# Attention output with V as the TensorE weights on four 128x32 column tiles, denominators in a second pass, and the projections of the same stages on column tiles

## The chip, the cores and the metric

The kernel runs on one core of one Trainium2 chip. The metric is the device time of one execution in microseconds (us). Three executions of the kernel before took 690.76, 691.12 and 691.33 us; their median is 691.12 us.

## What is computed

The reference is one transformer block in bfloat16 on 2048 tokens of width 1024: layernorm, attention with a sliding window, a residual, a second layernorm, a feed-forward layer with silu, and a residual. The attention has 32 heads of 32 channels, and each query sees itself and the 255 tokens before it.

```
qkv = layernorm(x) @ wqkv            # 1024 -> 3 * 1024
scores = q @ k.T * 32 ** -0.5        # per head
mask = (i - j >= 0) & (i - j < 256)  # i query, j key
p = softmax(where(mask, scores, -1e9))
h = x + (p @ v) @ wo
out = h + silu(layernorm(h) @ w1) @ w2   # w1: 1024 x 3584
```

## The kernel before

Tokens are handled in four blocks of 512 (b = 0 to 3). Heads are handled in groups of four (g = 0 to 7), because four heads of 32 channels fill the 128 partitions. After the projections of block 0 the kernel runs four **streamed stages** and then the feed-forward layer. In streamed stage b (0 to 3) the attention of block b is computed in small pieces between the matmuls of a dense projection: q, k and v of block b + 1 in stages 0 to 2, and the output projection `wo` of blocks 0 to 2 in stage 3. A stage has 24 dense groups of 8 matmuls, 128x128 weights by 512 columns (`v_group` L235, `qk_group` L244, `wo_group` L266; matmuls at L240, L250, L271), so 192 dense steps. Each dense group accumulates in one of two PSUM banks, `acc0` and `acc1`, and ends in one VectorE (DVE) instruction that empties the bank (L242, L252, L273).

The order of all engines is written out by hand (a manual schedule): each engine executes its instructions in the order in which the program emits them. Ahead of each dense step `Stream.between` (L434) is called. When a burst is due it first emits one waiting attention piece, then the burst of score matmuls, and then the dense step. Stage 0 has 16 bursts, so one comes every 12 dense steps; the stages after it have 20, five for each two head groups (one `scores_c` and four `scores_xy`), so one comes every 9.6 dense steps.

Score matmuls (L303, L329, L355) have the keys as weights, on tiles of 32 rows by 64 or 128 columns, and leave scores with keys on partitions and queries along the free dimension. ScalarE (ACT) takes exp of them into SBUF rings (L315, L316, L337, L363 to L365): `xy_ring` with two slots for each parity of the head group, and `c_ring` with three slots. GpSimd (POOL) then zeroes the triangles outside the window (`select`, L371 and L373).

The **attention output** of a head group (`attn_out`, L377; matmul at L383) has the probabilities as weights, 128x128, and V as the moving operand with 33 columns: 32 channels and a column of ones, so that column 33 of the result is the softmax denominator. Each group takes 48 such matmuls (16 outputs by three key tiles; 36 in block 0). The results for two heads lie in one PSUM bank (`o_ps`), with queries on partitions. `attn_norm` (L392) divides: a reciprocal of the 128x8 denominators (L394) and a multiplication of 128x256 (L395) into `obuf`. Then `attn_transpose` (L401) sends `obuf` through a DMA transpose on the SyncE (SP) queue to `qT`, where channels are on partitions, as `wo` needs them. There are two `o_ps` banks, one for each pair of heads.

In the last stage the pieces that remain are emitted between the first groups of the feed-forward layer. Layernorms are also emitted step by step between dense groups: that of block 2 in stage 0, that of block 3 in stage 1, none in stage 2, and the second layernorm of block 0 in stage 3.

Of the kernel before, what the change touches and what calls it, by code (L numbers as in the profile page):

```python
# [8 lines left out]
BF16 = mybir.dt.bfloat16  # L9
F32 = mybir.dt.float32  # L10
# [16 lines left out]
CHUNKS = [  # L27
    [(-2, "X", 0), (-1, "C", 0), (0, "X", 1)],
    [(-1, "Y", 0), (0, "X", 2), (1, "Y", 1)],
    [(0, "X", 3), (1, "Y", 2), (2, "X", 4)],  # L30
    [(1, "Y", 3), (2, "C", 1), (3, "Y", 4)],
]


CHUNKS_0 = [
    [(0, "X", 0)],
    [(0, "X", 1), (1, "Y", 0)],
    [(0, "X", 2), (1, "Y", 1), (2, "X", 3)],
    [(1, "Y", 2), (2, "C", 1), (3, "Y", 3)],
]  # L40
SPLIT = [(0, 8), (8, 16), (16, 21), (21, 27), (27, 32)]
# [3 lines left out]
def kernel(  # L45
# [23 lines left out]
    VW = DH + 1  # L69
# [15 lines left out]
    r_a = big.tile([P, 49664], BF16, name="r_a")  # L85
    r_e = big.tile([P, 13312], BF16, name="r_e")
    r_n = big.tile([P, 1536], BF16, name="r_n")
# [4 lines left out]
    o_ps = [ps.tile([P, 8, 64], F32, name=f"o_ps{i}") for i in range(2)]  # L92
# [24 lines left out]
    v = view(r_a, 32768, S // P, H, VW)  # L117
# [6 lines left out]
    obuf = [view(r_n, 512 * i, 4, P) for i in range(3)]  # L124
# [36 lines left out]
    nc.gpsimd.memset(v[:, :, :, DH:VW], 1.0)  # L161
# [4 lines left out]
    def busy(n):  # L166
        nc.tensor.matmul(o_ps[0][:].rearrange("p (a c) b -> p a (c b)", c=2)[:, 0:n], lhsT=warm, rhs=wide[:, 0:n], start=True, stop=True)  # L167
# [67 lines left out]
    def v_group(b, j, c, copy, between=None):  # L235
        acc = next_acc()
        for kt in range(KT):
            if between:
                between(kt)
            nc.tensor.matmul(acc, lhsT=lnT_b[b % 2][:, kt, j * P:(j + 1) * P], rhs=wv[:, kt, c * 512:(c + 1) * 512],  # L240
                             start=(kt == 0), stop=(kt == KT - 1))
        copy(out=v[:, b * 4 + j, c * 16:(c + 1) * 16, 0:DH], in_=acc.rearrange("p (h d) -> p h d", d=DH))  # L242

    def qk_group(b, which, g, copy, between=None):  # L244
        acc = next_acc()
        col0 = which * D + g * P
        for kt in range(KT):
            if between:
                between(kt)
            nc.tensor.matmul(acc, lhsT=wqk[:, kt, col0:col0 + P], rhs=lnT_b[b % 2][:, kt, :],  # L250
                             start=(kt == 0), stop=(kt == KT - 1))
        copy(out=(qT, kT)[which][b][:, g, :], in_=acc)  # L252
# [13 lines left out]
    def wo_group(b, j, c, between=None):  # L266
        acc = next_acc()
        for g in range(G):
            if between:
                between(g)  # L270
            nc.tensor.matmul(acc, lhsT=qT[b][:, g, j * P:(j + 1) * P], rhs=wo[:, g, c * 512:(c + 1) * 512],  # L271
                             start=(g == 0), stop=(g == G - 1))
        nc.vector.tensor_tensor(out=t_out[j % 2][:, c * 512:(c + 1) * 512], in0=acc,  # L273
                                in1=r_in[(b * 4 + j) % 6][:, c * 512:(c + 1) * 512], op=ALU.add)
        if c == 1:
            late.append(lambda: nc.sync.dma_start(out=h_dram[(b * 4 + j) * P:(b * 4 + j + 1) * P, :], in_=t_out[j % 2]))


    def chunk_of(i, bank, piece, pair, hh):
        if bank == "C":  # L280
            return c_ring[:, (i + 1) % 3, pair * 2 + hh, piece * P:(piece + 1) * P]
        if i < G:
            c0 = hh * 512 + piece * P
        else:
            c0 = 1024 + hh * P if piece == 2 else hh * 512 + (piece - piece // 3) * P
        return xy_ring[(i % 2 * 2 + "XY".index(bank)) * 2 + pair][:, c0:c0 + P]

    def scores_xy(b, g, odd):
# [20 lines left out]
        for pair in range(2):  # L309
            e = xy_ring[((b * G + g) % 2 * 2 + odd) * 2 + pair]  # L310
            tri = e[:, 0:1024].rearrange("p (h c q) -> p h c q", h=2, q=256)
            bank = sc[pair]
            both = bank[:, :, 0:192]
            both = bass.AP(tensor=both.tensor, offset=both.offset, ap=[*both.ap[:2], [320, 2], both.ap[2]])
            nc.scalar.activation(out=tri[:, :, :, 64:256], in_=both, func=ACT.Exp, scale=scale)  # L315
            nc.scalar.activation(out=e[:, 1024:1280].rearrange("p (h q) -> p h q", q=P), in_=bank[:, :, 192:320], func=ACT.Exp, scale=scale)  # L316
            four = e[:, 0:1024].rearrange("p (c q) -> p c q", q=256)
            select(four[:, :, 0:P], four[:, :, 64:64 + P], False)
            select(four[:, :, P:2 * P], four[:, :, P:2 * P], True)

# [19 lines left out]
    def scores_0(g, odd):  # L340
# [20 lines left out]
        for pair in range(2):  # L361
# [7 lines left out]
            select(e[:, :, 384:512], e[:, :, 384:512], True)  # L369

# [6 lines left out]
    def attn_out(b, g, first, last):  # L377
        i = b * G + g
        for n in range(first, last):
            pair, qt, hh = n // 8, n // 2 % 4, n % 2  # L380
            chunks = (CHUNKS if b else CHUNKS_0)[qt]
            for m, (kt, bank, piece) in enumerate(chunks):
                nc.tensor.matmul(  # L383
                    o_ps[pair][:, qt * 2 + hh, 0:VW],
                    lhsT=chunk_of(i, bank, piece, pair, hh),
                    rhs=v[:, b * 4 + kt, g * 4 + pair * 2 + hh, :],
                    start=(m == 0), stop=(m == len(chunks) - 1),
                )
            if n % 8 == 7:
                attn_norm(i, pair)  # L390

    def attn_norm(i, pair):  # L392
        recip = small.tile([P, 8, 1], F32, name="recip", tag="recip")
        nc.vector.reciprocal(out=recip[:], in_=o_ps[pair][:, :, DH:VW])  # L394
        nc.vector.tensor_tensor(  # L395
            out=obuf[i % 3][:, :, pair * 64:(pair + 1) * 64].rearrange("p t (h d) -> p t h d", d=DH),
            in0=o_ps[pair][:, :, 0:DH].rearrange("p (t h) d -> p t h d", h=2),
            in1=recip[:].rearrange("p (t h) o -> p t h o", h=2).to_broadcast([P, 4, 2, DH]), op=ALU.mult,
        )

    def attn_transpose(b, g):  # L401
        i = b * G + g
        nc.sync.dma_start_transpose(out=qT[b][:, g, :].rearrange("p (t q) -> p t q", q=P),
                                    in_=obuf[i % 3].rearrange("p t d -> p (t d)"))

    def attn_piece(b, g, first, last):

        for k in range(2):
            a, z = max(first - 16 * k, 0), min(last - 16 * k, 16)
            if a < z:  # L410
                attn_out(b, g + k, a, z)
                if z == 16:
                    late.append(lambda k=k: attn_transpose(b, g + k))

    class Stream:
# [3 lines left out]
        def __init__(self, b):  # L419
# [4 lines left out]
            for g in range(0, G, 2):  # L424
                if b:
                    self.bursts += [lambda g=g: scores_c(b, g)]
                    self.bursts += [lambda g=g, k=k, o=o: scores_xy(b, g + k, o) for k in range(2) for o in range(2)]
                    self.pieces += [lambda g=g, s=s: attn_piece(b, g, *s) for s in SPLIT]
                else:
                    self.bursts += [lambda g=g, k=k, o=o: scores_0(g + k, o) for k in range(2) for o in range(2)]  # L430
                    self.pieces += [lambda g=g, k=k: attn_piece(b, g, k, k + 8) for k in range(0, 32, 8)]
            self.n = len(self.bursts)

        def between(self, kt):  # L434
# [8 lines left out]
            self.seen += 1  # L443

# [37 lines left out]
    acc_banks += [o[:].rearrange("p a b -> p (a b)") for o in o_ps]  # L482
# [47 lines left out]
    for j in range(2):  # L530
        nc.scalar.activation(out=v[:, j, 16:32, 0:DH], in_=pair[j].rearrange("p (h d) -> p h d", d=DH), func=ACT.Identity, scale=rs[:, j:j + 1])
# [60 lines left out]
    dense = [lambda j=j, c=c: v_group(1, j, c, dve, stream.between) for j in range(4) for c in range(2)]  # L592
    dense += [lambda w=w, g=g: qk_group(1, w, g, dve, stream.between) for g in range(G) for w in range(2)]
# [10 lines left out]
    for b in range(2, NB):  # L604
        stream = Stream(b - 1)
        dense = [lambda j=j, c=c: v_group(b, j, c, dve, stream.between) for j in range(4) for c in range(2)]
        dense += [lambda w=w, g=g: qk_group(b, w, g, dve, stream.between) for g in range(G) for w in range(2)]
# [31 lines left out]
    for n in range(24):  # L639
# [3 lines left out]
        wo_group(*dense[n], stream.between)  # L643
# [5 lines left out]
        if n == 17:  # L649
            nc.sync.dma_start(out=w2[0], in_=w2_v[:, 0:4, :])  # L650
# [3 lines left out]
    pending += coming  # L654
# [27 lines left out]
    load_w2(5)  # L682
    for b in range(NB):
        extra = []
        if b == 0:
            extra = [(f, 1) for f in pending]
            pending = []
        for ft in range(FT):
            acc = h1_group(b, ft)
            run_late()  # L690
            if extra:
                extra.pop(0)[0]()
# [3 lines left out]
            silu(b, acc, ft)  # L696
            if b == 0 and 7 <= ft < 15:
# [61 lines left out]
```

## Time and profile before

| what | value |
|---|---|
| median of 3 runs (lowest to highest) | 691.12 us (690.76 to 691.33) |
| span of the profiled execution, first to last instruction | 688.9 us |
| PE (matmul) busy | 685.2 us, 6011 matmuls |
| DVE busy | 291.2 us |
| ACT busy | 244.2 us |
| POOL busy | 160.8 us |
| attention output matmuls, L383 | 1440 |
| score selects on POOL, L373 | 288, 157.8 us |
| attention transposes through DMA | 32, 2.3 us from issue to landing |

The profile is of one execution. Its own time is its span; the time that a run reports is measured around it, and the median of the runs is 2.2 us above this span. Busy time of PE counts an instruction from its start to its modelled end, and matmuls overlap, so a busy PE can still lose time between the starts of two matmuls. PEld stands for the loads of weights, which run beside matmuls.

### The profile page before, as it was taken

The page shows a single profiled execution, that of the slowest core. Times are in us where ns is not written, and L with a number is a line of the kernel's source. Part 1 is how long each engine was busy: PE and PEld are TensorE (multiplying, and loading weights), DVE is VectorE, ACT ScalarE, POOL GpSimd, SP SyncE. Part 2 cuts the span into 40 slices and gives each one's busy share as a digit, 9 for nine tenths or more (in the row PEclk, how much of TensorE's full clock was granted, in tenths as well). Part 3 has the DMA queues.
Part 4 walks back from the last instruction along what each step waited for, and adds up shares of the span by engine and source line. Part 5 has one row for each costly group of instructions (what it writes and reads, how often), then busy time and mean ns, then how long its engine had stood idle before and what let it go on. Part 6 is the DMA issues. An engine that isn't in the chain of part 4 may idle for free.

```text
span 688.9 us, 14243 instructions
## 1 busy us (share of the span) xinstructions
PE 685.2 (99%) x6011; PEld 342.3 (50%) x6011; DVE 291.2 (42%) x613; ACT 244.2 (35%) x464; POOL 160.8 (23%) x295
## 2 busy tenths in 40 slices
PE   9999999999999999999999999999999999999998
PEld 4445555555555555544444444444444444444445
DVE  5267647744444449444316133342233251333111
ACT  7326666666667666421300033300133100233000
POOL 1006666566666656400000000000000000000000
PEclk9999999999999999999999999999999999999999
DMA  7832231126241889871023310022300123100110
GB/s 259 275 64 69 40 85 57 25 63 186 71 131 21 257 252 272 199 267 40 23 88 112 84 39 0 1 91 70 85 0 1 21 96 90 39 1 1 30 39 24
DMA packets 78641, 61.48 MB, mean 89 GB/s; under 512 B 52465, under 2 KB 62705, under 8 KB 78577
## 3 DMA queue, kind: packets, MB, share of 16 engines
q1 hardware_dynamic: 77888, 59.78, 30.2%
q8 instruction: 47, 0.77, 0.4%
q10 hardware_dynamic: 688, 0.79, 0.3%
q14 instruction: 18, 0.14, 0.1%
HBM read 39.85 MB, written 8.39 MB: 70 GB/s over the span
## 4 chain that ended last, share of the span: by engine, by line
PE 99%; DVE 0%; issue 0%
PE hacc L669 19%; PE hacc L706 18%; PE acc L250 17%; PE acc L706 11%; PE acc L669 9%; PE acc L240 7%; PE acc L271 7%; PE o_ps L383 5%; PE sc L303 3%; PE hacc L271 2%; PE sc L355 1%; PE o_ps L240 1%; PE o_ps L167 1%; PE sc L329 1%; PE acc L525 0%; PE o_ps L525 0%
## 5 line engine op out<-in xcount | busy, mean ns | idle before, releaser
L373 POOL TENSOR_SCALAR_AFFINE_SELECT r_e<-r_e 128x512 bf16<-128x512 bf16 (+1 forms) x288 | 157.8, 563 | 123.9 <-ACT r_e L363 60.8
L706 PEld LDWEIGHTS <-r_a 128*128 128x128 bf16 x952 | 90.9, 98 | 103.0
L669 PEld LDWEIGHTS <-r_w 128*128 128x128 bf16 x896 | 87.3, 98 | 104.8
L706 PE MATMUL hacc<-r_a 128*128 128x512 bf16 (+2 forms) x616 | 122.5, 360 | 0.0
L669 PE MATMUL hacc<-r_e,r_w 128*128 128x512 bf16 x456 | 100.9, 379 | 0.0
L315 ACT ACTIVATE r_e<-sc 128x768 bf16<-128x768 f32 x96 | 78.2, 814 | 47.9 <-PE sc L303 47.9
L678 ACT ACTIVATE r_n<-hacc 128x512 f32<-128x512 f32 x30 | 17.9, 597 | 178.9 <-PE hacc L669 178.9
L250 PEld LDWEIGHTS <-r_w 128*128 128x128 bf16 x512 | 47.1, 98 | 55.0 <-issue 1.0
L706 PE MATMUL acc<-r_a 128*128 128x512 bf16 x336 | 74.0, 379 | 0.0
L252 DVE CAST r_a<-acc 128x512 bf16<-128x512 f32 x56 | 38.7, 692 | 57.7 <-PE acc L250 57.4
L250 PE MATMUL acc<-r_t,r_w 128*128 128x512 bf16 x256 | 59.6, 380 | 0.0
L250 PE MATMUL acc<-r_w 128*128 128x512 bf16 x256 | 57.8, 380 | 0.0
L383 PEld LDWEIGHTS <-r_e 128*128 128x128 bf16 x1440 | 47.4, 96 | 17.9
L669 PE MATMUL acc<-r_e,r_w 128*128 128x512 bf16 x216 | 49.1, 379 | 0.0
L271 PE MATMUL acc<-r_o,r_a 128*128 128x512 bf16 x208 | 48.7, 380 | 0.0
L383 PE MATMUL o_ps<-r_a,r_e 128*128 128x33 bf16 x1440 | 48.1, 178 | 0.0
L721 DVE SCALAR_TENSOR_TENSOR r_t<-hacc,r_t 128x512 bf16<-128x512 f32 (+2 forms) x22 | 14.0, 635 | 56.7 <-PE hacc L706 56.7
L316 ACT ACTIVATE r_e<-sc 128x256 bf16<-128x256 f32 x96 | 37.6, 392 | 0.0
L271 PEld LDWEIGHTS <-r_a 128*128 128x128 bf16 x256 | 23.4, 98 | 26.9
L721 DVE SCALAR_TENSOR_TENSOR r_t<-acc,r_t 128x512 bf16<-128x512 f32 x12 | 8.3, 692 | 64.2 <-PE acc L706 64.2
L679 DVE SCALAR_TENSOR_TENSOR r_a<-r_n,hacc 128x512 bf16<-128x512 f32 x30 | 20.6, 687 | 33.0 <-ACT r_n L678 33.0
L669 PE MATMUL hacc<-r_a,r_w 128*128 128x512 bf16 x144 | 33.0, 379 | 0.0
(100 smaller groups left out, 539.6 us busy)
## 6 DMA issues: line engine op xcount, KB each, us to landing
r_w<-in_B_w_dram SPq DMA_DIRECT2D x8, 896.0 KB, 5.2
r_a<-in_B_w_dram SPq DMA_DIRECT2D x7, 1024.0 KB, 7.5
r_w<-in_A_wqkv_dram SPq DMA_DIRECT2D x4, 1024.0 KB, 7.8
h_dram<-r_t SPq DMA_DIRECT2D x16, 256.0 KB, 3.1
r_t<-h_dram SPq DMA_DIRECT2D x16, 256.0 KB, 2.8
out_dram<-r_t SPq DMA_DIRECT2D x31, 128.0 KB, 1.7
r_o<-in_A_x_dram SPq DMA_DIRECT2D x15, 256.0 KB, 4.6
r_e<-h_dram SPq DMA_DIRECT2D x3, 1024.0 KB, 5.7
```

What stands on the lines that cost most here:

```text
L240: nc.tensor.matmul(acc, lhsT=lnT_b[b % 2][:, kt, j * P:(j + 1) * P], rhs=wv[:, kt, c * 512:(c + 1) * 512], start=(kt == 0), stop=(kt == KT ...
L250: nc.tensor.matmul(acc, lhsT=wqk[:, kt, col0:col0 + P], rhs=lnT_b[b % 2][:, kt, :], start=(kt == 0), stop=(kt == KT - 1))
L252: copy(out=(qT, kT)[which][b][:, g, :], in_=acc)
L271: nc.tensor.matmul(acc, lhsT=qT[b][:, g, j * P:(j + 1) * P], rhs=wo[:, g, c * 512:(c + 1) * 512], start=(g == 0), stop=(g == G - 1))
L303: nc.tensor.matmul(sc[hh // 2][half * 64:half * 64 + 64, hh % 2, col:col + qb - qa], lhsT=kT[t // 4][r0:r0 + DH, g, k0:k0 + 64], rhs=qT[b] ...
L315: nc.scalar.activation(out=tri[:, :, :, 64:256], in_=both, func=ACT.Exp, scale=scale)
L316: nc.scalar.activation(out=e[:, 1024:1280].rearrange("p (h q) -> p h q", q=P), in_=bank[:, :, 192:320], func=ACT.Exp, scale=scale)
L373: nc.gpsimd.affine_select(out=dst, in_=src, pattern=[[0, n] for n in dst.shape[1:-1]] + [[sgn, P]], compare_op=ALU.is_ge if upper else ALU ...
L383: nc.tensor.matmul(o_ps[pair][:, qt * 2 + hh, 0:VW], lhsT=chunk_of(i, bank, piece, pair, hh), rhs=v[:, b * 4 + kt, g * 4 + pair * 2 + hh, ...
L669: nc.tensor.matmul(acc, lhsT=w1[:, kt, ft * P:(ft + 1) * P], rhs=ln2T[b][:, kt, :], start=(kt == 0), stop=(kt == KT - 1))
L706: nc.tensor.matmul(acc[:, 0:c1 - c0], lhsT=gT[:, ft, j * P:(j + 1) * P], rhs=w2[ft // 4][:, ft % 4, c0:c1], start=(ft == 0), stop=(ft == F ...
L721: nc.vector.scalar_tensor_tensor(out=t_out[j % 2][:, c0:c1], in0=acc[:, 0:c1 - c0], scalar=0.5, in1=t_in[j % 2][:, c0:c1], op0=ALU.mult, o ...
```

## The change

V becomes the weight operand and the probabilities become the moving operand. The four heads of a group stand side by side on four column tiles of 128 rows by 32 columns: head h writes PSUM partitions 32h to 32h + 31. The result has channels on partitions, so it is already in the layout of `qT`, and the transposes through DMA and `obuf` are gone. The column of ones in V is gone too. The denominators come from a second pass over the probabilities with a 128x32 block of ones as weights, into the second `o_ps` bank; so they stand repeated on the 32 partitions of their head. The outputs are in `o_ps[0]` and the denominators in `o_ps[1]`, one bank each for a head group of 512 queries.

`V_STEPS` lists the first pass and `D_STEPS` the second (each entry: key tile or nothing, ring, first 128-column piece, how many pieces, and which query tiles). A step issues four matmuls, one for each head. To shorten the second pass the two triangles that cover a query tile are added beforehand on DVE (`sum_later`) into `both_tri`, two buffers that alternate between head groups. The sums are emitted 11 and 16 dense steps after their scores. After the second pass one reciprocal of 128x512 writes float32 into the first half of that group's `both_tri` buffer, and one multiplication of 128x512 writes `qT`.

The dense groups of the four streamed stages run on column tiles as well (`mm`, with `cols` = 32): each 128x128x512 matmul becomes four of 128x32 weights by the same 512 columns. The dense matmuls outside these stages stay as they are. In the tail, pieces still pending are emitted directly after stage 3, and the last three ahead of the fourth feed-forward group's silu. The load of `w2[0]` is emitted behind that of `w2[5]`, at the start of the feed-forward layer instead of in stage 3, since `both_tri` uses its place.

```diff
-CHUNKS = [
...
+V_STEPS = [
+    (0, "X", 1, 2, 0, 2), (1, "Y", 1, 2, 1, 2), (-2, "X", 0, 1, 0, 1), (-1, "C", 0, 1, 0, 1), (-1, "Y", 0, 1, 1, 1),
+    (0, "X", 8, 1, 1, 1), (1, "Y", 8, 1, 2, 1), (2, "X", 3, 1, 2, 1), (2, "C", 1, 1, 3, 1), (3, "Y", 3, 1, 3, 1),
 ]
-SPLIT = [(0, 8), (8, 16), (16, 21), (21, 27), (27, 32)]
+D_STEPS = [("F", 0, 2, 1, 1), ("C", 0, 2, 0, 3), ("M", 0, 4, 0, 1)]
+V_STEPS_0 = [(0, "X", 0, 3, 0, 1), (1, "Y", 0, 2, 1, 1), (1, "Y", 2, 1, 3, 1), (2, "X", 3, 1, 2, 1), (2, "C", 1, 1, 3, 1), (3, "Y", 3, 1, 3, 1)]
+D_STEPS_0 = [("Y", 0, 2, 1, 1), ("X", 0, 1, 0, 1), ("X", 1, 1, 1, 1), ("C", 1, 1, 3, 1), ("M", 2, 2, 2, 1)]
+SPLIT = [(0, 0, 8), (0, 8, 13), (1, 0, 5), (1, 5, 10), (1, 10, 13)]
+SPLIT_0 = [(0, 0, 5), (0, 5, 11), (1, 0, 5), (1, 5, 11)]
+TILE = 32
...
-    o_ps = [ps.tile([P, 8, 64], F32, name=f"o_ps{i}") for i in range(2)]
+    o_ps = [ps.tile([P, 512], F32, name=f"o_ps{i}") for i in range(2)]
...
-    obuf = [view(r_n, 512 * i, 4, P) for i in range(3)]
+    both_tri = [[view(r, o, 4, 4, P) for r, o in ((r_a, a), (r_n, 0))] for a in (0, 0, 18432, 18432)]
...
-    nc.gpsimd.memset(v[:, :, :, DH:VW], 1.0)
+    ones = const.tile([P, TILE], BF16, name="ones")
+    nc.gpsimd.memset(ones[:], 1.0)
...
+    def mm(acc, lhsT, rhs, start, stop, cols):
+        for c in range(0, P, cols):
+            tiled = {} if cols == P else {"tile_position": (0, c)}
+            nc.tensor.matmul(acc[c:c + cols, :], lhsT=lhsT[:, c:c + cols], rhs=rhs, start=start, stop=stop, **tiled)
...
+    def sum_later(i, odd, pair, out, in0, in1):
+        sums.append((clock[0] + 11 + 5 * pair, lambda: nc.vector.tensor_tensor(out=out, in0=in0, in1=in1, op=ALU.add)))
+
+    def run_sums(now):
+        while sums and sums[0][0] <= now:
+            sums.pop(0)[1]()
...
+            sum_later(b * G + g, odd, pair, both_tri[b][g % 2][:, pair * 2:pair * 2 + 2, odd::2, :], tri[:, :, :, 0:P], tri[:, :, :, P:2 * P])
...
+            sum_later(g, odd, pair, both_tri[0][g % 2][:, pair * 2:pair * 2 + 2, odd + 2, :], e[:, :, 256:384], e[:, :, 384:512])
...
+    def attn_piece(b, g, first, last):
+
         i = b * G + g
+        vs, ds = (V_STEPS, D_STEPS) if b else (V_STEPS_0, D_STEPS_0)
         for n in range(first, last):
...
+            kt, bank, p0, nb, q0, qs = vs[n] if n < len(vs) else (None, *ds[n - len(vs)])
+            m, total, acc = (n, len(vs), o_ps[0]) if n < len(vs) else (n - len(vs), len(ds), o_ps[1])
+            for head in range(4):
+                r0 = head * TILE
+                out = acc[r0:r0 + TILE, q0 * P:(q0 + 1) * P]
+                if nb > 1:
+                    out = bass.AP(tensor=out.tensor, offset=out.offset, ap=[out.ap[0], [qs * P, nb], out.ap[1]])
                 nc.tensor.matmul(
...
+                    out,
+                    lhsT=ones[:] if kt is None else v[:, b * 4 + kt, g * 4 + head, :],
+                    rhs=probs(i, bank, p0, nb, head),
+                    start=(m == 0), stop=(m == total - 1), tile_position=(0, r0),
                 )
...
+        if last == len(vs) + len(ds):
+            recip = both_tri[b][i % 2].rearrange("p a b c -> p (a b c)")[:, 0:1024].bitcast(F32)
+            nc.vector.reciprocal(out=recip, in_=o_ps[1][:])
+            nc.vector.tensor_tensor(out=qT[b][:, g, :], in0=o_ps[0][:], in1=recip, op=ALU.mult)
...
+                    self.pieces += [lambda g=g + k, s=s: attn_piece(b, g, *s) for k, *s in SPLIT]
...
+            clock[0] += 1
+            run_sums(clock[0])
...
+    dense = [lambda j=j, c=c: v_group(1, j, c, dve, stream.between, TILE) for j in range(4) for c in range(2)]
...
+        wo_group(*dense[n], stream.between, TILE)
...
-        if n == 17:
-            nc.sync.dma_start(out=w2[0], in_=w2_v[:, 0:4, :])
...
+    load_w2(0)
...
+            if b == 0 and ft == 3:
+                while coming:
+                    coming.pop(0)()
```

## Prediction before the run

> **What bounds the kernel now.** I read the page first, its busy times and the chain that ended last:
>
> ```profile
> PE 685.2 (99%) x6011; PEld 342.3 (50%) x6011; DVE 291.2 (42%) x613; ACT 244.2 (35%) x464; POOL 160.8 (23%) x295
> PE 99%; DVE 0%; issue 0%
> ```
>
> PE sets the end, and nothing else is on the chain. DVE is at 42%, but that is a mean, so next come the busy times by stage (streamed stages 0 to 3):
>
> ```profile
> core 0: us, PE busy (x) PEld busy (x) DVE busy (x) ACT busy (x) POOL busy (x), PEclk, DMA share, GB/s
> 49.20:104.30 55.10, 55.10 (x773) 29.70 (x766) 34.21 (x80) 35.07 (x96) 37.52 (x96) 1.00 0.32 76
> 104.30:164.40 60.10, 60.10 (x1014) 34.83 (x1014) 37.26 (x86) 40.79 (x72) 39.55 (x63) 1.00 0.20 47
> 164.40:224.50 60.10, 60.10 (x1028) 35.18 (x1026) 26.32 (x57) 40.79 (x72) 39.81 (x65) 1.00 0.36 110
> 224.50:283.70 59.20, 59.20 (x989) 34.40 (x986) 35.20 (x82) 40.58 (x72) 39.34 (x64) 1.00 0.92 254
> ```
>
> After the length of each stage stand PE, PEld, DVE, ACT and POOL. DVE has 21 to 34 us free in a stage, at full clock throughout. The timeline of PE gives the prices:
>
> ```profile
> 202.41 0.54 PE L383 MATMUL o_ps<-r_a,r_e 128*128 128x33 bf16 x15
> 202.89 0.43 PE L303 MATMUL sc<-r_a 32*64 32x320 bf16 x24
> 203.25 2.33 PE L250 MATMUL acc<-r_t,r_w 128*128 128x512 bf16 x10
> 205.41 0.76 PE L383 MATMUL o_ps<-r_a,r_e 128*128 128x33 bf16 x24
> ```
>
> Ten dense steps start at 203.25 and the next piece at 205.41: 0.216 us a step. Of 0.76 us for 24 attention matmuls the last one's own 0.178 is tail, so one costs 0.58 / 23 = 25.3 ns. From the last attention matmul's slot to the first dense one a score burst takes 0.45 us. Its 24 matmuls, on tiles of 32x64, would stream for 1.73 us in series (8 each of 320, 128 and 64 columns, at 0.216/512 us a column). They take 0.43 less a tail of 0.16, 0.27 us: over six times less, more than the four row groups can give, so the two column tiles of a row group run at once. The last rows are DVE's, of all shapes apart:
>
> ```profile
> L252 DVE CAST r_a<-acc 128x512 bf16<-128x512 f32 x56 | 38.7, 692 | 57.7 <-PE acc L250 57.4
> L395 DVE TENSOR_TENSOR r_n<-o_ps,recip 128x256 bf16<-128x256 f32 x64 | 27.2, 424 | 2.2
> L174 DVE BATCH_NORM_STATS2 ln_st<-r_o 128x6 f32<-128x512 bf16 x28 | 17.8, 678 | 0.0
> L394 DVE RECIPROCAL recip<-o_ps 128x8 f32<-128x8 f32 x64 | 12.8, 200 | 30.1 <-PE o_ps L383 29.9
> L212 DVE RECIPROCAL rs_a<-rs_a 128x1 f32<-128x1 f32 x4 | 0.5, 143 | 0.3 <-ACT rs_a L209 0.3
> ```
>
> **PE's part.** In stages 1 to 3 a head group gives up 48 x 25.3 ns = 1.21 us and takes on 12 + 8 pieces of 128 columns for four heads at once: 2560 columns x 0.42 ns = 1.08 us. In stage 0 it is 36 x 25.3 = 0.91 against 2048 columns = 0.86. Together 24 x 0.13 + 8 x 0.05 = 3.6 us saved. A dense step of four 128x32 matmuls I take at 0.216 us as before: same columns, and tiles overlap in the row above. The score bursts keep their two changes of tile shape. In the tail, 72 matmuls of 25.3 ns (1.8 us) become 13 steps (1.1 us) and two changes of shape at about 0.1: 0.4 us. So PE alone saves 4 us.
>
> **DVE's part.** Out go 64 reciprocals and 64 multiplications (40 us). In come 32 reciprocals of 128x512, 32 multiplications of 128x512, 96 sums of 128x512 and 32 of 128x256.
> - Multiplication: L395 is 0.424 for 256 elements, L252 0.692 for 512 from PSUM: 0.69 us.
> - Sum: no row shows it. From below a 128x256 bf16 operation (0.28 us, L468), from above a row of one element a cycle (L174, 0.68). I take 0.5; each 0.1 moves the total by some 7 us, since sums stand ahead of other work.
> - Reciprocal of 128x512: not in the trace, and it decides. If it runs like L252, 0.69 us. But L252 and L395 both fit 0.158 us plus 1.04 ns an element, by which L394's 8 elements would take 0.166. Where DVE was idle before it, its records read 0.207 to 0.209, so 0.05 us is over, and a strided read is no reason: L395 reads the same bank with gaps and fits. It is no fixed price either, as L212 takes 0.143. So it goes by the element: 0.05/8 = 6.1 ns, and 512 of them make 3.1 + 0.16 = **3.3 us**. With all of (0.207 - 0.143)/7 put on an element, 9.1 ns, it is 4.8 us. Ends: 0.69 and 4.8. I take 3.3, from the row of the same operation on PSUM.
>
> [...]
>
> **The new wait.** Before, two `o_ps` banks were freed by 0.2 + 0.42 us of DVE work each. Now a head group's outputs have one bank, so the next group's first V matmul waits for the multiplication behind the reciprocal, and on PE's queue every dense step stands behind that matmul. Between a group's last denominator step and the next group's first V step PE has one burst and 9.6 dense steps: 0.45 + 9.6 x 0.216 = 2.5 us (stage 0: 12 steps, 3.0). DVE needs the last matmul's tail past its slot (0.38 - 0.216 = 0.16), 0.04 to start, 3.3, 0.03, 0.69 and some 0.05 back to PE: 4.3, and about 0.4 for the copy or sum it is in. So PE stops for 4.7 - 2.5 = 2.2 us a group in stages 1 to 3 and 1.7 in stage 0: 24 x 2.2 + 8 x 1.7 = **66 us**.
>
> DVE itself is then nearly full: a group takes 3.3 + 0.69 + 4 x 0.5 + 3 copies x 0.69, 8.1 us, of a period of 7.4 ((60.1 - 1) / 8) + 2.2 = 9.6. Where a layernorm is in the stage, 11 us more come in (37.3 less 10 for the old division and 16.6 for 24 copies), 1.4 a group: no slack is left, and its pieces of 1.6 us (two L174 and the aggregate) stand ahead of reciprocals and bank copies. I charge 7.5 us each in stages 1 and 3 and 3 in stage 0, where a group has half a microsecond more cover: **18 us**.
>
> **What costs nothing.** 32 transposes leave SP's queue and nobody waits for them. The load of `w2[0]` is now behind the load of `w2[5]` and waits for group 6 of block 3, some 5 us into the feed-forward layer; only weights used 60 us later stand behind it. Group 7 of block 3 ends in the fourth feed-forward group; `wo` needs it four groups (6.9 us) later, and 4.3 fits. ACT and POOL get no work, and slower stages give them more room.
>
> **Sum.** 688.9 - 4 + 66 + 18 = 769 us of span. The median of the runs stands 2.2 above this span, so **771 us**.
>
> **Rivals.**
> - The reciprocal runs at one cycle an element (0.69 us). Then the chain is 1.7 + 0.4 us, under the 2.5 of cover. Left are the layernorm's pieces: 1.6 ahead makes 3.7, a stop of 1.2 us some eight times. 691 - 4 + 10 = 697. Against it: L394.
> - The other side, faster: the same, and the layernorm pieces fall clear of the divisions, so only PE's 4 us count: 687. The mechanism is that the chain hides under a burst and 9.6 steps; it decides at a reciprocal of 2.5 - 0.97 - 0.4, about 1.1 us or less. For it: DVE's 21 to 34 us free. Against: L394 and the blocks of 1.6 us.
> - The change doesn't do what it says: four column tiles on all 128 rows read the same columns four times, while the score tiles show two streams per row group. If two run at a time, a dense step is 0.432, a stage has 41 us more, and the chain hides under 4.6 us of cover: 691 + 4 x 41 = 855. [...]
>
> **How the numbers follow.** Slow reciprocal (771): 0.80. One cycle, slower (697): 0.07. One cycle, faster (687): 0.09. Tiles two at a time (855): 0.04. Within the first case a reciprocal at 8 ns an element gives 32 x 1.0 us more (803), sums of 0.3 or 0.7 give 14 less or more, and fewer collisions leave out half of the 18 and more. Its range is 730 to 815, which leaves out 0.2; the ends of the reciprocal lie at 697 and, at 4.8 us, at 819. A measurement of this kernel tells about 0.2% from no change. Faster: 0.09; same: 0.01, between the two one-cycle cases; slower: 0.90.
>
> **What would show it.** The reciprocal's row at 3.3 us for 128x512; PE waiting for DVE's multiplication some 30 times for 60 to 80 us in all; stages of some 71, 84, 77 and 83 us; dense groups still 0.216 us from step to step. Wrong would be: a reciprocal near 0.7 us, or PE without waits and with longer steps, or a clock below 1.00 in the stops, which I haven't counted.

## The result, and the profile after

The changed kernel took 765.06 us, the median of 4 runs (764.26 to 767.01); the kernel before, on the same chip, 690.94 us (690.76 to 691.33). The ratio is **1.1073, with an interval of 1.1056 to 1.109**. The forecast was 771 us, slower, for a division that is slow on DVE; the range 730 to 815 holds the result.

The profiled execution took 765.63 us, with a span of 763.9. First come lines of its page: the busy times, the rows of 40 slices for DVE and for PE's clock, and the shares of the chain that ended last.

```profile
PE 700.5 (92%) x8434; PEld 338.1 (44%) x8475; DVE 425.6 (56%) x677; ACT 244.1 (32%) x464; POOL 162.1 (21%) x295
DVE  4278888888888888998643162432413325134211
PEclk9999999799999999989999999999999999999999
PE 76%; DVE 21%; issue 2%; DMA 1%; ACT 0%; ACTq 0%; DVEq 0%
```

Before, the chain was PE alone. Now a fifth of it is DVE, which is busy for 80% or more of slices 4 to 19, the streamed stages, though its mean over the span is only 56%. The busy times by stage (columns as in the prediction) show where the time went:

```profile
core 0: us, PE busy (x) PEld busy (x) DVE busy (x) ACT busy (x) POOL busy (x), PEclk, DMA share, GB/s
49.75:119.92 70.17, 59.60 (x1397) 30.14 (x1396) 57.07 (x96) 35.07 (x96) 37.36 (x96) 0.95 0.22 56
119.92:204.01 84.09, 66.54 (x1628) 34.44 (x1624) 70.38 (x100) 40.80 (x72) 40.68 (x64) 0.92 0.16 46
204.01:277.83 73.82, 61.03 (x1638) 32.38 (x1635) 62.12 (x73) 40.80 (x72) 41.26 (x65) 1.00 0.13 42
277.83:359.05 81.22, 65.58 (x1637) 34.04 (x1633) 71.98 (x101) 40.79 (x72) 40.97 (x65) 0.94 0.57 165
```

The stages are bounded by their first score bursts, and the last one by the first matmul of the feed-forward layer. By the same bounds those of before took 55.1, 60.1, 60.1 and 59.4 us. So the four stages are longer by 74.6 us, which is nearly the whole loss: the time up to them grew by 0.9, and the rest went from 405.4 to 404.9 us. PE's waits (total us, times, longest) give most of it to one place, the first V matmul of a head group, which waits for the multiplication:

```profile
PE o_ps L401 <- DVE r_a L410: 54.1, 29, 3.4
PE acc L233 <- DVE r_a L241: 2.4, 1, 2.4
```

The groups of DVE's operations give the reason. The reciprocal is L409, the multiplication L410, the sum of two triangles L292:

```profile
L409 DVE RECIPROCAL r_n<-o_ps 128x512 f32<-128x512 f32 x16 | 53.6, 3350 | 5.5 <-PE o_ps L401 5.5
L409 DVE RECIPROCAL r_a<-o_ps 128x512 f32<-128x512 f32 x16 | 53.5, 3342 | 0.0
L292 DVE TENSOR_TENSOR r_n<-r_e 128x512 bf16<-128x512 bf16 x48 | 23.7, 515 | 0.0
L410 DVE TENSOR_TENSOR r_a<-o_ps,r_n 128x512 bf16<-128x512 f32 x16 | 11.1, 691 | 0.6
```

One cycle of it, from the chain in stage 2 (start, length, what):

```profile
212.16 2.06 PE acc L233 x36
214.22 0.46 PE o_ps L401 x12
214.68 0.02 issue
214.70 3.37 DVE r_n L409
218.07 0.02 issue
218.09 0.70 DVE r_a L410
218.80 0.04 issue
218.84 0.74 PE o_ps L401 x32
```

The twelve matmuls at 214.22 are the second pass of one head group. The first V matmul of the next one starts at 218.84, 4.62 us later. In between PE had a burst and nine or ten dense steps to do, and then stood still for the rest.

### The profile page after: what moved, and what is told of

It is laid out like the page before. It is cut to its first block, busy times and chain, and to the rows that moved or that the text cites. A ratio compares the mean times of both kernels' runs of the same rounds, so it can differ in the third digit from the quotient of the medians.

```text
span 763.9 us, 19203 instructions
## 1 busy us (share of the span) xinstructions
PE 700.5 (92%) x8434; PEld 338.1 (44%) x8475; DVE 425.6 (56%) x677; ACT 244.1 (32%) x464; POOL 162.1 (21%) x295
## 4 chain that ended last, share of the span: by engine, by line
PE 76%; DVE 21%; issue 2%; DMA 1%; ACT 0%; ACTq 0%; DVEq 0%
PE acc L233 17%; PE hacc L667 17%; PE hacc L704 16%; PE acc L704 9%; PE acc L667 8%; DVE r_n L409 7%; DVE r_a L409 7%; PE o_ps L401 4%; DVE r_a L410 2%; PE sc L313 2%; DVE ln_st L169 1%; PE hacc L233 1%; DVE r_a L250 1%; DMA r_w<-in_A_wqkv_dram 1%; PE o_ps L233 1%
## 5 line engine op out<-in xcount | busy, mean ns | idle before, releaser
L667 PEld LDWEIGHTS <-r_w 128*128 128x128 bf16 x896 | 87.5, 98 | 105.9 <-issue 0.6
L233 PEld LDWEIGHTS <-r_w 128*32 128x32 bf16 (+1 forms) x1968 | 62.8, 100 | 70.3 <-issue 11.8
L233 PE MATMUL acc<-r_w 128*32 128x512 bf16 (+1 forms) x917 | 82.7, 398 | 3.5 <-DVE r_a L241 2.4
L401 PE MATMUL o_ps<-r_e,r_a 128*32 128x128 bf16 (+2 forms) x1152 | 33.1, 244 | 54.1 <-DVE r_a L410 54.1
L233 PE MATMUL acc<-r_t,r_w 128*32 128x512 bf16 x1024 | 62.9, 394 | 0.0
L401 PEld LDWEIGHTS <-r_a 128*32 128x32 bf16 x1152 | 24.0, 101 | 77.1 <-DVE r_a L410 68.4
L409 DVE RECIPROCAL r_n<-o_ps 128x512 f32<-128x512 f32 x16 | 53.6, 3350 | 5.5 <-PE o_ps L401 5.5
L409 DVE RECIPROCAL r_a<-o_ps 128x512 f32<-128x512 f32 x16 | 53.5, 3342 | 0.0
L233 PE MATMUL acc<-r_o,r_a 128*32 128x512 bf16 (+1 forms) x784 | 52.5, 402 | 0.0
L233 PEld LDWEIGHTS <-r_a 128*32 128x32 bf16 (+1 forms) x832 | 25.7, 100 | 27.7 <-issue 3.6
```

The costliest lines, as they stand in the source:

```text
L233: nc.tensor.matmul(acc[c:c + cols, :], lhsT=lhsT[:, c:c + cols], rhs=rhs, start=start, stop=stop, **tiled)
L401: nc.tensor.matmul(out, lhsT=ones[:] if kt is None else v[:, b * 4 + kt, g * 4 + head, :], rhs=probs(i, bank, p0, nb, head), start=(m == 0 ...
L409: nc.vector.reciprocal(out=recip, in_=o_ps[1][:])
L667: nc.tensor.matmul(acc, lhsT=w1[:, kt, ft * P:(ft + 1) * P], rhs=ln2T[b][:, kt, :], start=(kt == 0), stop=(kt == KT - 1))
```

## The experiments

Each kernel is the changed one with one edit, or the one before with one part of the change. Times are medians, the ratio is to the kernel before (690.9 to 691.2 us beside them), and the stages are those of the profiled execution.

| kernel | us (lowest to highest) | ratio (95%) | stages 0 to 3, us |
|---|---|---|---|
| the change | 765.1 (764.3 to 767.0) | 1.1073 (1.1056 to 1.109) | 70.2, 84.1, 73.8, 81.2 |
| e1_copy | 700.7 (699.3 to 702.0) | 1.0137 (1.0121 to 1.0154) | 55.9, 64.1, 59.6, 66.0 |
| e2_half | 712.5 (709.3 to 716.5) | 1.0311 (1.0272 to 1.0351) | 57.6, 69.0, 61.0, 69.2 |
| e3_cover | 786.0 (783.3 to 786.8) | 1.1362 (1.1337 to 1.1387) | 68.1, 84.3, 87.5, 88.6 |
| e4_cover_actcopy | 734.0 (731.9 to 735.1) | 1.0616 (1.0597 to 1.0635) | 56.5, 67.6, 66.4, 86.1 |
| e8_actcopy | 752.5 (751.8 to 754.2) | 1.0893 (1.0877 to 1.0909) | 63.7, 77.4, 73.6, 81.8 |
| e7_copy_actcopy | 696.8 (695.7 to 699.5) | 1.0089 (1.0065 to 1.0112) | 55.2, 59.9, 59.6, 67.1 |
| e6_copy_nosums | 703.7 (701.0 to 705.4) | 1.0179 (1.0154 to 1.0205) | 56.3, 63.3, 62.2, 65.5 |
| e5_copy_dense128 | 705.1 (704.6 to 705.9) | 1.0205 (1.0188 to 1.0222) | 57.2, 65.9, 61.7, 64.6 |
| e9c_before_tiles | 703.9 (703.3 to 704.9) | 1.0186 (1.017 to 1.0201) | 56.7, 62.3, 63.5, 64.6 |
| e10c_ln | 700.9 (698.9 to 703.5) | 1.0144 (1.0113 to 1.0174) | 55.1, 63.4, 61.3, 65.6 |
| e11c_ln_dense128 | 703.5 (703.1 to 704.7) | 1.0183 (1.0166 to 1.02) | 56.6, 63.8, 62.6, 64.4 |

**The price of the division.** Two kernels make it cheaper and leave all else in place.

```diff
-            nc.vector.reciprocal(out=recip, in_=o_ps[1][:])
+            nc.vector.tensor_copy(out=recip, in_=o_ps[1][:])
```

> The reciprocal is replaced by a copy of the same 128x512 (so outputs are multiplied by the denominators instead of divided by them); nothing else is changed. Theory: nearly all of the 74 us is PE waiting behind the 3.35 us reciprocal. A copy from PSUM takes 0.69 us, so 32 x 2.66 = 85 us less DVE work; the chain of 1.7 to 2.1 us fits under the 2.5 us of cover, the waits of 54 us go, the half clock in the stops goes with them, and some 10 us of stops stay where a layernorm piece stands ahead: 690 to 700 us, dense steps 0.217 us as in the changed kernel. Rival (the column tiles themselves are dear): at least a third of the loss stays, over 715 us.

The copy takes 0.68 us, the kernel 700.7 us, and PE's wait for L410 shrinks from 54.1 us to 4.3 in three waits:

```profile
PE o_ps L401 <- DVE r_a L410: 4.3, 3, 1.8
```

So 64 of the 74 us come from the reciprocal's length, the half clock that follows the stops included (30.7 us of it in the stages of the changed kernel, 3.4 here). Some 10 us do not.

```diff
-            nc.vector.reciprocal(out=recip, in_=o_ps[1][:])
+            nc.vector.reciprocal(out=recip[:, 0:256], in_=o_ps[1][:, 0:256])
...
```

> The reciprocal is taken of 256 of the 512 columns, and both halves of the queries are multiplied by it (so queries 256 to 511 of a block get the wrong denominators). Theory: the price goes by the element, so the row reads 0.16 + 256 x 6.2 ns = 1.75 us, and each of 32 groups gains the 1.6 us while a stop lasts: about 714 us, with short stops of 0.3 to 0.5 us left. Rival (a fixed price of the instruction, or the wait is for something else): the row stays near 3.3 us or the time stays above 745 us.

The multiplication here reads the 256 results twice. The reciprocal's group:

```profile
L409 DVE RECIPROCAL r_n<-o_ps 128x256 f32<-128x256 f32 x16 | 28.0, 1750 | 5.1 <-PE o_ps L401 5.1
```

1750 ns for 256 elements and 3350 for 512 make 6.25 ns an element and 0.15 us fixed, which gives the old 128x8 form 0.20 us, as its row had. The loss is not proportional to the length. From 0.68 to 1.75 us DVE gets 34 us more work and the kernel 11.8 us more time; from 1.75 to 3.35 it is 51 us of work for 52.6 of time. In stage 2, where no layernorm runs, the first step costs 1.4 us for eight groups and the second 12.8. That is the shape of a cover. Below some 1.6 us (an estimate: 3.35 less the 1.8 us that a group of stage 2 loses) the division hides under PE's burst and dense steps. Above it each group of stage 2 pays the whole difference: 12.8 / 8 is 1.6 us, as 3.35 - 1.75. In the other stages the time also has the clock in it, at half for 30.7 us in the change and for 6.8 in e2_half.

**More cover.** The second pass is put earlier, so that two bursts and their dense steps, not one, lie between it and the next group's V.

```diff
-SPLIT = [(0, 0, 8), (0, 8, 13), (1, 0, 5), (1, 5, 10), (1, 10, 13)]
-SPLIT_0 = [(0, 0, 5), (0, 5, 11), (1, 0, 5), (1, 5, 11)]
+SPLIT = [(0, 0, 13), (0, 0, 0), (1, 0, 5), (1, 5, 13), (1, 0, 0)]
+SPLIT_0 = [(0, 0, 11), (0, 0, 0), (1, 0, 11), (1, 0, 0)]
```

> The pieces are dealt anew over the same bursts, so that two bursts and some 19 dense steps (5 us; 6 us in stage 0) lie between the end of a group's second pass and the next group's first V step, instead of one; no instruction is added or left out. Theory A, as in the prediction (the wait is for the single output bank): the chain of 4.7 us fits under 5 us and the 54 us of waiting go, some 700 us. Theory B (DVE's queue in order is the limit, the bank is only where it shows): the copies of the dense banks then stand behind the reciprocal, PE stops at acc instead of o_ps, each bank having 2.9 us of cover, and the time stays at 760 to 775 us.

It became slower, 786 us. PE's waits:

```profile
PE acc L233 <- DVE r_a L250: 31.2, 17, 2.2
PE acc L233 <- DVE r_t L270: 14.2, 7, 2.4
PE acc L233 <- DVE r_a L241: 11.7, 8, 2.4
```

No wait for L410 is left among them. The stop has moved to the dense groups: both `acc` banks are full, and the copy or addition that empties one stands on DVE behind the reciprocal, as in these rows of DVE's timeline in e3_cover, after which PE goes on at 204.49:

```profile
199.42 3.36 DVE L409 RECIPROCAL r_a<-o_ps 128x512 f32<-128x512 f32 x1 [0.48 <-PE o_ps L401]
202.82 0.69 DVE L410 TENSOR_TENSOR r_a<-o_ps,r_a 128x512 bf16<-128x512 f32 x1
203.42 0.41 DVE L292 TENSOR_TENSOR r_n<-r_e 128x512 bf16<-128x512 bf16 x1
203.76 0.68 DVE L250 CAST r_a<-acc 128x512 bf16<-128x512 f32 x1
```

The mechanism is as expected; the time is over the 760 to 775 us. What that left out is the clock: PE's granted clock was 0.5 for 51 us of its stages and the steps after them, against 31 in the changed kernel. By PE's work in those windows I put that at 25 us, an estimate. Without it the time would be 761 at the least, since slower dense steps are also longer cover.

So a second kernel also moves the bank copies of stages 0 to 2 to ACT, and a third moves only them.

```diff
-... v_group(1, j, c, dve, stream.between, TILE) ...
+... v_group(1, j, c, act, stream.between, TILE) ...
```

> As the run with doubled cover, and the copies of the dense q, k and v banks of stages 0 to 2 are made by ACT (0.59 us each, 14 us a stage on an engine with 18 us free) instead of DVE. Theory B: now neither the output bank nor the dense banks stand behind the reciprocal, DVE has 6.2 to 7.6 us of work in a group's 7.4: 700 to 712 us, stages 0 to 2 near 57, 65 and 62 us, and stage 3, whose additions stay on DVE, longer. Theory A: no different from the run with doubled cover alone. If ACT becomes the limit, PE stops at sc, and the time is over 725 us.

> The changed kernel with its reciprocal, cover as in the change, only the q, k and v banks of stages 0 to 2 emptied by ACT: the fourth corner beside the changed kernel (765), doubled cover (786) and both (734). If the two waits (output bank, dense banks) stand one behind the other, this alone gives back little: the chain of 4.3 us against 2.5 us of cover stays, only the copies ahead of the reciprocal go: 740 to 757 us, PE waiting at o_ps. If DVE's amount of work is the limit, it gives as much as both together: 730 to 737 us.

The copies alone give 752.5 us, as expected, and PE still waits for the division (first line below, from the waits of e8_actcopy). Cover and copies together give 734: cover alone cost 21 us, and beside the copies it gains 18.5. It is still not the 700 to 712 expected; the second fence has waits of e4_cover_actcopy.

```profile
PE o_ps L401 <- DVE r_a L410: 51.1, 29, 4.5
```

```profile
PE acc L233 <- DVE r_t L270: 11.8, 6, 2.2
PE o_ps L401 <- DVE r_a L292: 6.0, 15, 1.2
```

There are three things behind the reciprocal on DVE's queue, each awaited by PE: the bank copies, the sums that the next second pass reads (L292), and in stage 3 the additions into the residual (L270), which that edit left on DVE. The sums stand there four in a row: in stage 2, at 191.17 us, four of them took 1.42 us, and the mean of that stage is some 0.5 us (an estimate: DVE's 49.4 us less eight divisions and multiplications of 4.05, for 33 sums). Stage 3 is 86 us, the others 56 to 68. One wait was removed and the next in the same queue took its place, twice.

**What is left when the division costs nothing.** Four kernels look into the 10 us of e1_copy. The first adds the ACT copies to it:

> As the run with a copy in place of the reciprocal (outputs multiplied by the denominators), with the q, k and v banks of stages 0 to 2 emptied by ACT. DVE then has slack everywhere but in stage 3. If the saving of 4 us that was worked out for PE is real, it shows here: stages 0 to 2 at 54.7, 59 and 59 us (55.1, 60.1 and 60.1 before the change), stage 3 near 62 to 66: 690 to 696 us. If not: no stage below its time before the change.

Stages 0 to 2 come to 55.2, 59.9 and 59.6 us, against 55.1, 60.1 and 60.1 before. In stage 1 of e1_copy PE waited 2.5 us for the multiplication and 0.6 for a bank copy; here it waits 0.1. So most of the 4 us that e1_copy loses there come from DVE having both the bank copies and the layernorm's pieces in its queue. And with almost nothing in its way PE's own gain is 0.5 us in stage 2 and 0.7 in three stages. Stage 3 stays at 67.1 us against 59.4. In it PE has three stops that no semaphore releases (below), 3.0 us in all, and one wait of 1.8 for the multiplication, after which its clock is halved for 3.4 us.

The next drops the sums; the second pass then has as many steps as the first.

```diff
-D_STEPS = [("F", 0, 2, 1, 1), ("C", 0, 2, 0, 3), ("M", 0, 4, 0, 1)]
+D_STEPS = [s[1:] for s in V_STEPS]
...
-        sums.append((clock[0] + 11 + 5 * pair, lambda: nc.vector.tensor_tensor(...)))
+        return
...
```

> As the run with a copy in place of the reciprocal (outputs multiplied by the denominators), and the second pass streams all twelve pieces (nine in stage 0) instead of adding triangles on DVE first. PE pays 4 x 53 ns for 24 groups and 2 x 53 for 8, 6 us; DVE has 57 us less. Theory (what is left of the loss is DVE's work in the stages with a layernorm colliding): stages 1 and 3 fall from 64 and 66 to some 62, stage 2 rises from 59.6 to 61: 694 to 699 us. Rival (what is left is PE's own price): 705 to 708 us.

It did not come to the expected 694 to 699 us. Stages 1 and 3 fell by only 0.8 and 0.5 us against e1_copy and stage 2 rose by 2.6, so the sums are not most of what remains. Its PE has stops that no semaphore releases (the profile calls them "issue"): at 252.78 us a dense step of four matmuls starts, and the next step only at 254.50. In each of four such stops, 0.9 to 1.7 us from start to start, a packet of 16 KB of the instruction queue ("q8 instruction" among the page's DMA queues) ran or had just ended.

That points at the column tiles, which make four instructions of one. Two kernels test them. One takes them out of e1_copy (`cols = P` in `mm`), the other puts only them into the kernel before.

> As the run with a copy in place of the reciprocal (outputs multiplied by the denominators), with the projections of the streamed stages put back on 128x128 weights; the attention stays on 128x32 tiles. Theory: a dense step costs 0.217 us either way, and what the column tiles of the projections buy is only that no change of tile shape stands between a dense step and an attention piece: some 76 changes of 0.1 us more, so 703 to 712 us against 700.7. Rival (four matmuls for one, with four loads of weights, are dearer somewhere): under 699 us.

> The kernel before, with its own attention (probabilities as weights, transposes through DMA) and only the projections of the streamed stages put on four 128x32 tiles. Dense steps stay at 0.217 us. Theory on the stops without a release (PE's instruction stream runs dry: four times the dense instructions, and each stop stands beside a 16 KB instruction packet that lands inside it): they appear here too, without any attention change, 2 to 6 of 0.8 to 1.7 us, in stage 3 above all, where DMA is 92% busy; with one more change of shape at each of some 75 pieces (0.1 us): 698 to 707 us. Rival (those stops belong to the new attention's waits): no stop over 0.45 us, 697 to 700 us.

Both lose, for different reasons. Without tiles the stops are gone and the instruction queue carries 48 packets (before: 47; the changed kernel: 66), but 128x128 dense steps beside 128x32 attention matmuls change the tile shape: the start of the next attention piece comes 309 ns after that of the last dense step, not 216 as in the kernel before, where both are 128x128. The kernel is 4.4 us slower than e1_copy. The kernel before with tiles is 12.8 us slower than without them. In it the full-width attention matmuls come 312 ns after the last of a dense step's four matmuls, where the changed kernel has 207; 18 times a stage that makes 1.9 us. It also has 65 packets and stops again: three of 0.4 us and this one of 1.7 inside a score burst (PE's timeline; a packet ran from 269.86 to 270.80):

```profile
270.08 0.41 PE L305 MATMUL sc<-r_a 32*64 32x320 bf16 x18
272.21 0.23 PE L305 MATMUL sc<-r_a 32*64 32x64 bf16 x6 [1.73 <-issue]
```

So tiles for the projections pay only because the attention output is on tiles too. That the stops are late instructions is argued from their place beside the packets and from their absence in the kernels with 48; no run shows PE waiting for a fetch. Nor do many packets always bring such a stop: the changed kernel, e3_cover and e8_actcopy have 66 each and none, but there PE also waits for DVE in nearly every group.

**Another way to divide.** ACT computes exp(-ln d) where DVE took the reciprocal, with both functions from the one table set that the kernel loads ahead of the stages (of e10c_ln's three table loads of 1.28 us none stands at L410 or L411); the last head group keeps the reciprocal.

```diff
-            nc.vector.reciprocal(out=recip, in_=o_ps[1][:])
+            if i < 4 * G - 1:
+                nc.scalar.activation(out=recip, in_=o_ps[1][:], func=ACT.Ln)
+                nc.scalar.activation(out=recip, in_=recip, func=ACT.Exp, scale=-1.0)
+            else:
+                nc.vector.reciprocal(out=recip, in_=o_ps[1][:])
...
+    nc.scalar.preload_act_table_set("natural_log_exp_and_others")
```

> The changed kernel with the reciprocal taken off DVE: ACT computes exp(-ln(d)) with two instructions of 128x512, about 0.6 us each, from one table set that holds both; only the last head group keeps the reciprocal. Theory: what is dear is where the 3.35 us stand, not the division as such. DVE has 107 us less; ACT has 1.2 us more for each group, ahead of the next burst's exps, so PE stops briefly at sc: 700 to 710 us. Rival (any division between the two passes costs the chain): over 730 us.

> As the run with exp(-ln(d)) on ACT (700.9), with the projections back on 128x128 weights: fewer instructions (no stops for instructions in stage 3), one more change of shape a piece. By the pair measured with the copy (700.7 and 705.1) some 3 to 5 us above the run with tiles: 704 to 710 us. If stops for instructions are worth more than the changes of shape when DVE is not the limit, it is below that run.

ACT's groups and PE's longest wait in e10c_ln:

```profile
L410 ACT ACTIVATE r_a<-o_ps 128x512 f32<-128x512 f32 x16 | 9.6, 597 | 9.0 <-PE o_ps L401 9.0
L411 ACT ACTIVATE r_a<-r_a 128x512 f32<-128x512 f32 x16 | 10.1, 632 | 0.5
```

```profile
PE o_ps L401 <- DVE r_a L414: 2.7, 3, 1.4
```

Two operations of 0.6 us on ACT do what took 3.35 us on DVE, and the kernel takes 700.9 us, inside the 700 to 710 expected. PE's short stops at the scores came as expected: in stage 2 they make the score bursts 1.7 us longer in all than in e1_copy, which is the 1.7 by which that stage is longer. That is the full computation at the price of e1_copy, and the confirmation that the division's place and length, not the new layout, cost the 64 us. With plain dense steps it is 703.5, half a us below the 704 to 710 expected. None of these kernels is faster than the one before.

## Why the prediction was right, point by point

- **The reciprocal, 3.3 us.** Right: 3.35. The 50 ns that L394 was over the fixed 0.158 us of the other rows were a price per element, 6.25 ns. (Over the line itself, 0.166 for 8 elements, it was 41 ns; the prediction divides the 50, as it should for the whole price of an element.) The same price stands in the 128x256 row of e2_half. No run shows the 8 ns an element from which the prediction's range takes 803 us; these two rows give 6.25. What the prediction and its rivals call one element a cycle is 512 elements in 0.68 to 0.69 us (L174 and L252); no run shows a cycle of DVE.
- **The multiplication and the sums.** 0.691 against 0.69; 0.51 against 0.5. Single sums in one stretch of stage 2 took 0.41 to 0.83 us.
- **The wait in stages without a layernorm.** Predicted 2.2 us a group; in stage 2 the eight waits are 12.8 us, 1.6 each. The profile counts a wait from the modelled end of the last matmul, 0.38 us after its start, while a dense step's slot is 0.21; in lost slots, as the prediction counts, it is 14.2 us, 1.8 each. The cycle above shows where the 0.4 went: from the reciprocal's start to V it is 4.14 us, nearly the 4.1 worked out, but the 0.4 us for an operation that the reciprocal arrives behind fell away. In all eight cycles of stage 2 it starts 0.43 us after the last denominator matmul's start where DVE was idle, and 0.49 where a bank copy stood ahead. The stage, predicted at 77 us, is 73.8.
- **The layernorm's collisions, 18 us.** The step that was mis-sized. Stage 1 waits 17.5 us, and stage 3 15.6, against 12.8 in stage 2: 4.7 and 2.8 more, not 7.5 each. Stage 0 waits 10.6 us, which is below the 13.6 charged for it without a layernorm. That "no slack is left" on DVE did not hold either: DVE was idle for 13.7 us of stage 1 and 9.2 of stage 3. All waits come to 56.5 us, or 61.7 in lost slots, where 66 + 18 were charged.
- **The clock in the stops.** Named as not counted, and it came. In the changed kernel's stages PE was granted 0.5 for 30.7 us, in seven windows, none of them in stage 2. Two dense stretches from the chain, the first right after a stop in stage 0, the second in stage 2 of the same execution:

```profile
70.19 4.42 PE acc L233 x48
...
227.71 2.27 PE acc L233 x40
```

  Ten steps take 2.27 us at full clock, so twelve in 4.42 are some 1.7 us late. By PE's work in the seven windows I put the whole at 14 us, an estimate. It falls into stages 0, 1 and 3, where the layernorm was overcharged; slower dense steps are also longer cover, so the two may be linked. That link was not tried. Two errors of opposite sign, 22 us too much wait and 14 too little for the clock, bring the total near. That 771 came within 6 us of the result is in part luck; that the kernel is slower, and by the wait behind the reciprocal, is not.
- **PE's saving, 4 us.** Wrong in size: about 0.5 us a stage where it could be seen (e7_copy_actcopy), not 1.0. The streaming was right: in stage 2 of the change steps of 128 and 256 columns start 56 and 109 ns apart, where the price of 0.42 ns a column makes 53 and 107. Part of what failed is "the score bursts keep their two changes of tile shape": from the attention's last matmul to the burst's first it was 107 ns before, 82 over the 25 of a matmul, and is 150 now after 128 columns or 312 after 512, some 95 over the streaming. At 19 pieces a stage that is 0.25 us of the missing 0.5; the rest of it is open. In stage 3 the stops without a release take more than was saved.
- **The dense step.** Right: 0.217 us with four 128x32 tiles, before and after. The tiles stream side by side, and the rival at 855 us falls.
- **The free items.** Right as far as shown: PE has no wait for `w2[0]` or `wo`, and the feed-forward layer took 404.9 us.
- **The rivals at 697 and 687.** Their mechanism was tested by e1_copy, which has an operation of 0.68 us in the division's place: 700.7, near the slower one of the two. That was 3.7 us low; the changes of shape, the stops and a window of half clock (at 281 us) were not in it.

Sum, against 75.0 us more span: 61.7 of lost slots and 14 of clock make 76, less some 0.7 of PE's saving (three stages of e7_copy_actcopy) and 0.5 in the feed-forward layer, plus 0.9 for the later start of the stages. It closes to within 1 us.

## What to carry to other kernels

A row with few elements hides its price per element in what looks like a fixed cost (here 8 elements of 6.25 ns, 0.05 us of a row of 0.20): fit the other rows of the engine first, and price the excess by the element before the operation is made 64 times as large. Then ask what stands behind the long operation on its queue, since widening the cover of one wait (e3_cover) only brings up the next, here three deep; moving the operation to an engine that does it in 1.2 us (e10c_ln) did more than all rescheduling. An engine with 21 to 34 us free in a stage is free only for operations shorter than the cover that one buffer gives, here some 1.6 us of division.

## What the runs showed of the hardware

- PE's clock was halved for 3.413 us (five windows of the change) or twice that (two), beginning 2.5 to 5.1 us after the start of a stop of 2.1 to 3.8 us (between the starts of two matmuls) in the change, in four of seven windows with PE busy again. In e3_cover stops of 2.1 to 2.6 us stand ahead of most of its 15 windows. But the length alone does not decide: in the change eight stops of 2.0 us in stage 2 brought none, and four of 2.1 to 2.7 us elsewhere (at 88, 122, 158 and 353 us) brought none either.
- The windows lie on a grid. The seven starts in the change (70.67, 80.92, 135.53, 145.77, 169.66, 330.09 and 343.74 us) are whole multiples of 3.413 us apart. Cut into cells by this grid, each window of the change follows a cell in which PE lost 1.93 to 2.81 us in stops, and no other cell at full clock lost more than 1.91 us (starts of two matmuls over 0.45 us apart, less the slot of 0.21). In the change it was the loss within one cell that parted the two, not the length of a single stop; in e10c_ln two stops of 1.2 and 1.4 us in one cell stood ahead of a window. What sets the grid was not shown. In e3_cover the border is less sharp: 1.7 to 2.9 us ahead of windows, up to 1.9 elsewhere.
- Four 128x32x512 matmuls on column tiles take the time of one of 128x128x512 (0.217 us); a change from 128x128 steps to 128x32 attention matmuls costs 93 ns (309 against 216, e5_copy_dense128), one from 128x32 steps to 128x128 some 105 (312 against 207, e9c_before_tiles).
- With 65 to 72 packets of 16 KB on the instruction queue in place of 47, PE stood still for 0.8 to 2.6 us from start to start, once to four times in an execution, with no release that the profile shows and such a packet running or ended up to 0.7 us before (e1_copy, e2_half, e4_cover_actcopy, e6_copy_nosums, e7_copy_actcopy, e9c_before_tiles and e10c_ln; not in the change, e3_cover and e8_actcopy).
